# Block-sparse attention with a gated convolution behind it: the same operations in another written order

## The chip, the core and the metric

The kernel runs on one core of a Trainium2 chip. The core has five engines that run at the same time, each of them its own instructions in the order in which they were written: TensorE (PE in the profile; its weight loads are listed as PEld), VectorE (DVE), ScalarE (ACT), GpSimd (POOL) and SyncE (SP). TensorE multiplies matrices and writes to PSUM; VectorE and ScalarE read PSUM and compute; GpSimd writes constants and starts loads; SyncE starts transposing transfers and stores. Engines wait for each other only where one needs the data, or the buffer, of another. The metric is the device time of the whole program in microseconds (us).

## The reference

q, k and v have the shape (4, 8, 768, 64): 4 batches, 8 heads, 768 tokens, 64 values per head. The sequence is cut into 24 blocks of 32 tokens.

```python
scores = scale * np.matmul(q, k.transpose(0, 1, 3, 2))          # scale = 1 / sqrt(64)
mask = np.abs(blk_i - blk_j) <= 1
mask = mask | (blk_i == 0) | (blk_j == 0) | (blk_i == 23) | (blk_j == 23)
for qb in range(24):
    for kb in sampled_blocks[qb]:                               # 3 of them
        mask[qb*32:(qb+1)*32, kb*32:(kb+1)*32] = True
attn = softmax(np.where(mask, scores, -1e9))                    # written out in the reference
x = (attn @ v).transpose(0, 2, 1, 3).reshape(4, 768, 512)       # the heads side by side
h = np.maximum(x @ w_in, 0.0)                                   # 512 -> 1024
conv_out[t] = sum over k of conv_w[k] * h[t + k - 1]            # 3 taps, each channel by itself
out = h * sigmoid(conv_out) @ w_out                             # 1024 -> 512, float32
```

## The kernel before

**Attention.** The mask is not added to the scores but multiplied in with them: a tile T (`t` in the profile) holds, for two heads, the transposed q and k in 64 rows and 24 more rows that encode the mask, so that one matmul over 88 rows gives the masked score. Two heads are a *pair*; there are 16 pairs, four per batch. Attention is cut into 144 *units* of 8 blocks of 128 × 128 scores. For each unit TensorE makes the scores (L755, into one of two PSUM buffers `st`), ScalarE takes the exponential (L767, `pt<-st`, 1024 columns, six `pt` buffers), and TensorE multiplies with V, which has a column of ones beside it for the row sum (L792, into one of two buffers `av`). When the four or so units of a pair are done, VectorE takes the reciprocal of the row sums (L700, `rcp<-av`) and normalizes (L702, `xtok<-av,rcp`), and the tokens are transposed into `xT`.

**Feed-forward.** The tokens are worked on in segments of 384 (the last one as 256 and 128). For each segment and each of eight groups of 128 channels TensorE multiplies with w_in (L889, `mix<-xT,winb`, into one of two PSUM buffers `mix`), and the relu takes the result out of `mix`, on ScalarE (L909) or on VectorE (L911). VectorE makes the three taps (L947 and L955), ScalarE the tanh that serves as sigmoid (L994), VectorE the gate (L997 and L1002). Then TensorE multiplies with w_out (L824, `mix<-woutb,gT`), the result is copied to `o2s` by ScalarE (L327) or VectorE (L331), and SyncE stores it. The work of the feed-forward for one segment is strewn among the units of the next, so that all engines have both kinds of work all the time; only the last segment has its feed-forward with no attention beside it (the tail). In the last segment the taps are matmuls on TensorE (L966).

**Loading.** GpSimd starts all loads that change float32 into bfloat16 on the way (helper `dma`, L238): k and q into `nat` (four buffers) or `nq` (four), v into `vn` (three buffers). Pairs 0 to 5 are transposed by TensorE; pairs 6 to 15 by transposing transfers that SyncE starts (L596, `stg<-nat`, two `stg` buffers) and then two copies `t<-stg` of 64 × 1536 values each, on VectorE or ScalarE. V is copied from `vn` into its place (`vt<-vn`, VectorE, L331). So that the loads don't all start at once, GpSimd executes small copies between them, called *pace*, which wait for the exponential of a given unit (L407) or for the landing of an earlier load (L666).

**Start.** VectorE zeroes `warm` and `ident` (L222, L223). TensorE runs 13 warming matmuls and then 32 *fill* matmuls of 128 columns (L229), which go between the first real ones and whose results are not used. GpSimd makes an index pattern (L260), the identity matrix (L262, a select over the zeroed `ident`), the same in float32 (L286, L287), the ones column of each of the five V tiles (L359, `vt<-`), and the zeros at both ends of the two `hE` buffers that hold h (L364 and L365).

**Order.** The program is a graph of 1789 operations. Each has a name, the engines on which it can run, and the buffers that it takes; some hold several instructions. The numbers beside them (durations, due times `T(u)`) decide nothing any more: `put_down` reads a string, `ORDER`, and issues the operations in the order written there. An entry is two characters for the operation (its number in base 64), one letter for the engine where there is a choice (P, A, V, G, S for TensorE, ScalarE, VectorE, GpSimd, SyncE), and one character for each buffer that it takes. Waits follow from the tiles that operations share, so a string of another order gives a correct program with other waits:

```python
o = ops[64 * CODE.index(line[x]) + CODE.index(line[x + 1])]
...
if len(engines) > 1:
    e = ENGINES[line[x]]
...
for b in o.allocs:
    b.index = CODE.index(line[x])
...
    o.fn(e)
```

Of the kernel before, what the change touches and what calls it, by code (L numbers as in the profile page):

```python
# [25 lines left out]
2u6x11p6y6c6d1u6h6z16i06C06j26D6k6q2W6r6v6E46w1+V6L11ZV6M4Z4R6A1l2H06B6l16N26Q05VV6R2I6mV6F6G6S52a16H26V16I6W323
6O16P2bV6X06J06+01x6KV6T6/2cV6Uid07041b73174ig11s755ieihifV0d7b0iiA7c2GV17g17h7d1iB22o1ij0iDik7i36Y2pV6Z7l0ilV7
7m712qV727n2767q1iC7rim0781iEin7s033797y07z2v1ioV7a27A47717D12UV37EiJ17e7f7j7F52wV47I03507J2y0iL7k7K17o7N12xV7O
7p2Z7t2AV7u7P3iK7S07T7v22J14WiF4U7U04+4O7+12X14T2KV07/1v7B07CiM7G8027H8303902LV7L7M847QiG3012zV2M17R7w7V8818514V
892NV1y7x7W1ip0iN81iq2OV8a08d01q8eis1iH8f482irVeit368l1iI08687iO8b7X18miuViv07Y8q08n28riP8c7Ziy1iR3iz8s5iTiw3o2  # L30
# [5 lines left out]
adaejV2aias1ap19WatjWjz1jXjAau3ax0jYay3tjDjTaz2aj1jZaqaC1aravak0jEVaD9zjBAaK0alaE0awaLk10aAkr1k3am2aM4aBkf0aP1k2
jUaFaQj+3A2aGk43r4aN0aU0aR5aO4/ksk53Y3D0kgj/k63IaVk03LaS4YaZ14aaTaW4a+k7kt3J2khk8a/5b203Cku3M3b3kiaX3iV3uVkvA13Z
aYba1b42b0aH2bb3jV3Bb1kx1bc33E1kjV33Obf0bg3N3vVkybh0kJ03P0b5kKb70aIbk1kzA10kLVbblbp0bqbm11rb61aJkA13VV1kM03yV2
br4bdbe3Tbx1by3FkNbz2kBkOVbibjbnbobsbC0l92kCA3QbDlbbH1bE5kG0b8kS1kTlab9bIkV1kUAbM0bNbJ1kWbtkD1bA0bu1jgkXkEbO3kk
kHkFVgbR1bBbFkIA3KV3bS4B3bGlcbKbT4bZ0b+l10bLkP0kYkQb/5ldbPbQkl1kZc21lec3bvbUkmc423HVbwbV1c0l2c70c8k+kn3RV13/4y1  # L40
ko3SVkRA2c1cc14bbW0cdc954003GVc5c6k904n2l3kakpA34Cck0bXce4cacbcll44QbY0kb3+k/cm1kcl53W4k0cfcgcp1l01l6cqcu0kdV2
lE1cr0lFlh3kecvcn0li4cco4e1lH0lGAl7cz1cw5cAlklIljlK1cscB4lL48lJV4DcE0llctcFlMA41cxlfcy45cG2cM14om51cNcCcDlv1cO5
kwcR0l8cScHlB0lgcT0lC4dm6m7lwcW1ch0lmcXcic/0d0cJ1lDAlx4lV4cY4lncI1lZ0cPcQcUcVlolp04pd12d71l+d84M0lyl/d93dc0dd4E
m0m8lqde0cZ4jdh1462lrm9lzA0dicKc+lsmam1lA504qd2d3da0ltV1cLdm0dj5lN1mbdnlOd42m2d5dbkqlQ0lPVdr1ludo3lRm3df4fdslSV
dgdt1lT1dkm4dz0dAmd2dlcjlW0dB4melXmfdplUlYAmgdqd6dE14rlVA4mdFmcdudv1dG0dCml0dJ0dKmmmz0dL2mhdDdHdO1dImomAmimndPdM
# [5 lines left out]
oqfB0nLnIfCorfG1fD3osot4JVfHnQfI1frnMnRnSnNV1oufL0fMnTV3nV1fN5fsovnWnUft2nY0ownZnXAfufQ0n+AfRf7fY1fS4fZfz0oh0f81
o80oio51f+0ojo6g10o9okfvo7Ag2oaVfAfEfFg32g61fJolfKnOox3fOg7fPomfToyfU1f/ob0oAocg84gb0ozoe1onofodAgcooogAg0g4g5oB
gd0gj1oT0oF1gkoN1oGoCoHgo0gpgl5g9fV0gaoIoOfWoUgq1oJgefXgt1gfoDguoKgm0gnoEgC0grgDgv2gsoLoVgg2oMoPgE5ghgH1oWgigI
oXA2gwgxgM0gNoQoRV3p30gO4p4gy0oSgzp5gJ34Kp6gV0p7A1oYgWpc1pdgX0p90pagF0gGpbV11peAg+1g/h30px1gKh05gLgA1pypi0h4gBV0
gPpzgQh52gY1pjgR0pApf1pgpkApBgZh1phA4hc1gSh2pCh6hdpF0gT1hh0gUVh7he4po0pGhipHpl1hj3pmpIpppnVdhm1hnpqAh80hv0pJpu1
ho0pDpvpN3hf0hghkpwApr0h9pKhwpE0pspOhlhpptAghA1pPhqhx3ha1hBhr0oZ0pQo+hshbAhC0o/hy1pRhzht1pV1p0pSpWhJ1huVhKp1A2pX
hS0qg1pYpLhL3p2hDqhpTqm0pZqiA0qnpUp+qd1hF2pMhTqoAehX1hGhE0hMqx0hU4qehNqyp/hYq10qfA7hO0hPq2hZ3q0i40hH1qAi5q3qp1
hIA1i62qzq4qqhV1hWh+q5A0qBqj1qsqrqCh/0q6i7hQ0i8qkhRAp8i91i02iaq70i1qlA2qN2q8qF3ib1q9icAqPi21qaqHi3Are1qGqbA2rfqt
rgAqOqcr50qur6qIr81r7Arw0qDrxqvr9qErh1riraAqwrb0qJrj0rcq/1rkrdAqQrm1qKrnrlr0qRry0rB0qLro1qMqSrr0rsrT1rpr1rqrt3rz
rH0qTrurCrvrIrJrAqUrDrKrErLA2rUr2rFA0rN0rVr3A1rWrGqV0rXArMqWrYrOrPrQqXrRVqYrSr4qZA3q+  # L60
"""


# [987 lines left out]
```

## Time and profile before

| | |
|---|---|
| time, median of 3 runs | 208.37 us (207.83 to 209.8) |
| the profiled execution | 208.56 us, of which its span in the profile 206.8 us |
| TensorE busy (matmuls) | 197.9 us, 96% |
| ScalarE busy | 190.5 us, 92% |
| VectorE busy | 183.3 us, 89% |
| GpSimd busy | 59.9 us, 29% |

The span is from the first to the last instruction that the profile shows; the program's own time is 1.76 us longer. Times inside the profile count from the start of the span. The views used below are: the page (shares and the chain that ended last), the stretches (busy time of each engine between two points of time; the columns are the stretch, its length, PE, PEld, DVE, ACT, POOL with numbers of instructions, the granted TensorE clock, the share of the DMA engines and GB/s), the list of waits (engine, what waited, for what; total us, how often, the longest), the timeline of one engine (start, busy time, engine, line, operation, output and inputs, count; in brackets the idle time before it and what ended it), and the groups of equal instructions (count; busy us and mean ns of one; idle time before them).

### The profile page before, as it was taken

What the parts mean: (1) busy time and instruction counts of PE and PEld (TensorE: products, weight loads), DVE (VectorE), ACT (ScalarE), POOL (GpSimd) and SP (SyncE); (2) the same over time, 40 slices, a digit from 0 to 9 for tenths busy, and PEclk for the clock granted to TensorE, in tenths of its full rate; (3) what the DMA queues carried; (4) which work ended last, traced back from release to release, by engine and by line L of the source; (5) the groups of instructions that cost most, each with busy time, mean ns of one, the idle gap of its engine ahead of it and who ended that gap; (6) DMA issues with size and microseconds to landing.
All of it is one profiled execution on the core that took longest, in us unless ns stands there. A gap on an engine that the chain in (4) does not pass through costs nothing.

```text
span 206.8 us, 6166 instructions
## 1 busy us (share of the span) xinstructions
PE 197.9 (96%) x2397; PEld 143.3 (69%) x2417; DVE 183.3 (89%) x561; ACT 190.5 (92%) x251; POOL 59.9 (29%) x125
## 2 busy tenths in 40 slices
PE   7899999999979999999999999999999999999992
PEld 5688877877647766776666766776657768787761
DVE  6889899999969999699999998999899929999940
ACT  6999999999988999999999998999899988999751
POOL 8793950800890037411956120000000000000000
PEclk9999999999999999999999999999999999999999
DMA  6999999999699995998999911563213030011205
GB/s 154 147 176 151 146 177 196 136 200 172 77 128 194 179 137 74 168 142 198 120 209 194 243 30 38 67 141 104 101 52 92 19 97 34 3 52 54 103 3 203
DMA packets 51113, 25.40 MB, mean 123 GB/s; under 512 B 36780, under 2 KB 48140, under 8 KB 51084
## 3 DMA queue, kind: packets, MB, share of 16 engines
q0 software_dynamic: 20000, 11.24, 44.6%
q1 hardware_dynamic: 30796, 13.46, 32.8%
q8 instruction: 19, 0.31, 0.7%
q10 hardware_dynamic: 288, 0.30, 0.5%
q14 instruction: 10, 0.08, 0.2%
HBM read 23.09 MB, written 6.29 MB: 142 GB/s over the span
## 4 chain that ended last, share of the span: by engine, by line
PE 66%; DVE 14%; ACT 8%; DMA 6%; issue 3%; POOL 1%; SPq 0%; DVEq 0%
PE st L755 20%; PE mix L889 15%; PE mix L824 14%; PE av L792 11%; ACT pt L767 5%; DVE t L331 4%; DVE m L947 3%; DMA stg<-nat 3%; DMA vn<-in_v_dram 3%; DVE hE L911 2%; DVE m L955 2%; PE av L229 2%; ACT t L327 1%; ACT m L994 1%; PE st L824 1%
## 5 line engine op out<-in xcount | busy, mean ns | idle before, releaser
L767 ACT ACTIVATE pt<-st 128x1024 bf16<-128x1024 f32 (+1 forms) x145 | 140.7, 1027 | 5.1 <-PE st L755 4.4
L755 PE MATMUL st<-t 88*128 88x256 bf16 (+2 forms) x600 | 91.6, 268 | 1.5 <-ACT pt L767 0.8
L792 PEld LDWEIGHTS <-pt 128*128 128x128 bf16 x1152 | 55.5, 97 | 14.6 <-issue 0.2
L792 PE MATMUL av<-vt,pt 128*128 128x65 bf16 x1152 | 62.2, 193 | 0.3
L755 PEld LDWEIGHTS <-t 88*128 88x128 bf16 x600 | 48.0, 97 | 20.6 <-issue 2.8
L889 PE MATMUL mix<-xT,winb 128*128 128x384 bf16 (+2 forms) x288 | 54.1, 308 | 1.8 <-DVE hE L911 1.5
L947 DVE TENSOR_SCALAR m<-hE,cw 128x382 bf16<-128x382 bf16 (+2 forms) x192 | 49.0, 316 | 0.4 <-ACT hE L909 0.2
L824 PE MATMUL mix<-woutb,gT 128*128 128x512 bf16 x164 | 46.1, 379 | 0.4
L955 DVE TENSOR_TENSOR m<-m 128x764 bf16<-128x764 bf16 (+2 forms) x64 | 33.6, 532 | 0.4
L889 PEld LDWEIGHTS <-winb 128*128 128x128 bf16 x288 | 23.7, 97 | 9.6 <-issue 2.4
L994 ACT ACTIVATE m<-m 128x764 bf16<-128x764 bf16 (+2 forms) x32 | 26.3, 826 | 0.1
L824 PEld LDWEIGHTS <-gT 128*128 128x128 bf16 x208 | 17.6, 97 | 10.0 <-issue 0.2
L407 POOL COPY pace<-pt 1x1 bf16<-1x1 bf16 x24 | 6.8, 284 | 44.6 <-ACT pt L767 44.4
L909 ACT ACTIVATE hE<-mix 128x384 bf16<-128x384 f32 (+2 forms) x38 | 18.7, 501 | 1.1 <-PE mix L889 1.0
L1002 DVE TENSOR_TENSOR gT<-m,hE 128x764 bf16<-128x764 bf16 (+3 forms) x36 | 18.0, 510 | 1.0 <-ACT hE L909 0.7
L702 DVE TENSOR_TENSOR xtok<-av,rcp 128x384 bf16<-128x384 f32 (+2 forms) x36 | 18.1, 507 | 0.4
L911 DVE TENSOR_SCALAR hE<-mix 128x384 bf16<-128x384 f32 x26 | 14.2, 552 | 3.9 <-PE mix L889 3.6
L238 POOL DMA_DIRECT2D nat<-in_q_dram x23 | 17.1, 744 | 0.7 <-issue 0.5
L238 POOL DMA_DIRECT2D vn<-in_v_dram x16 | 11.7, 733 | 9.2 <-DVE rcp L700 4.7
L238 POOL DMA_DIRECT2D nat<-in_k_dram x15 | 10.8, 724 | 11.5 <-DMA stg<-nat 7.7
L331 DVE COPY t<-mix 64x384 bf16<-64x384 bf16 (+1 forms) x30 | 12.2, 418 | 0.6 <-ACT t L327 0.2
L997 DVE TENSOR_SCALAR m<-m 128x764 bf16<-128x764 bf16 (+3 forms) x36 | 11.8, 337 | 0.4 <-ACT m L994 0.3
(79 smaller groups left out, 121.2 us busy)
## 6 DMA issues: line engine op xcount, KB each, us to landing
out_dram<-o2s SPq DMA_DIRECT2D x23, 256.0 KB, 2.5
vn<-in_v_dram POOLq DMA_DIRECT2D x16, 192.0 KB, 5.6
nat<-in_k_dram POOLq DMA_DIRECT2D x15, 192.0 KB, 5.8
nat<-in_q_dram POOLq DMA_DIRECT2D x6, 192.0 KB, 6.5
winb<-in_moe_w_in_dram POOLq DMA_DIRECT2D x2, 512.0 KB, 10.0
woutb<-in_moe_w_out_dram POOLq DMA_DIRECT2D x4, 256.0 KB, 7.5
nat<-in_q_dram POOLq DMA_DIRECT2D x9, 96.0 KB, 5.5
nq<-in_q_dram POOLq DMA_DIRECT2D x6, 96.0 KB, 5.1
```

The costliest lines, as they stand in the source:

```text
L238: return op(name, {eng: occ}, lambda e: on(e).dma_start(out=dst(), in_=src), prio, deps, dma=(kind, service), **kw)
L331: nc.vector.tensor_copy(out=dst, in_=src)
L755: nc.tensor.matmul(out=st[:, 128 * x:128 * (x + n_)], lhsT=t[0:88, 12 + 6 * hh + kc, :], rhs=t[0:88, idx:idx + (n_ - 1) * (2 if P < NPE el ...
L767: nc.scalar.activation(out=pt_t[ptb.index][:, c0:c1], in_=st_t[stb.index][:, c0:c1], func=AF.Exp, bias=0.0, scale=0.125)
L792: nc.tensor.matmul(out=o[:, off:off + 65], lhsT=pt_t[ptb.index][:, 128 * x:128 * x + 128], rhs=V_t[vslot_b[P].index][:, hh, kc, 0:65], sta ...
L824: nc.tensor.matmul(out=acc(), lhsT=gT_t[gb.index][:, ffc, 128 * t:128 * t + 128], rhs=woutb[:, ffc, c0:c1], start=(ffc == 0), stop=(ffc == ...
L889: nc.tensor.matmul(out=mix_t[hb.index][:, w1 * y:w1 * y + w1], lhsT=winb[:, fc, 128 * ffc:128 * ffc + 128], rhs=xT_t[xt_buf[n].index][:, f ...
L909: nc.scalar.activation(out=dst, in_=src, func=AF.Relu, bias=0.0, scale=0.5)
L911: nc.vector.tensor_scalar(out=dst, in0=src, scalar1=0.5, scalar2=0.0, op0=ALU.mult, op1=ALU.max)
L947: nc.vector.tensor_scalar(out=m_t[cb.index][:, x, y, 0:w], in0=hE_t[heb.index][:, f0 + y, t0 + x:t0 + x + w], scalar1=cw[:, x, f0 + y:f0 + ...
L955: nc.vector.tensor_tensor(out=m[:, a_, :, 0:w], in0=m[:, a_, :, 0:w], in1=m[:, b_, :, 0:w], op=ALU.add)
L994: th = [op("tanh", {"ACT": t_act(2 * w) + 0.04}, lambda e, cb=cb, w=w: nc.scalar.activation(out=m_t[cb.index][:, 0, :, 0:w], in_=m_t[cb.in ...
```

## The change

Only the string `ORDER` differs: the same 1789 operations in another order, with other engine letters in 22 of them and other buffer numbers. In each engine's own sequence, 729 of TensorE's 894 operations stand at another place than before, 193 of ScalarE's 252, 372 of VectorE's 441, 108 of GpSimd's 118 and 8 of SyncE's 84; most of them by a few places.

What the entries say, where it can be put in words:

- GpSimd's start. Before: identity, index pattern, three ones columns, first k load, two more columns between the first loads, and the zeros of `hE` after the loads (at 7.34 and 15.92 us). After: one ones column (`1c`), index pattern (`0R`), identity (`0S`), zeros of the first `hE` (`1h`), a ones column, zeros of the second `hE` (`1i`), a ones column, and then the first k load (`1P`); the two other columns follow behind that load.
- TensorE's start. Eight more of the fill matmuls stand ahead of the first real ones.
- Around 60 us on VectorE. Before: reciprocal, two copies of transposed q, the copy of pair 8's V (`3mV`), normalization (`96`), two relus (`jmV`, `jjV`). After: reciprocal, normalization, the two copies of q, the first relu, pair 8's V, the second relu. The V copy of pair 7 (`3aV`) moves from 51.5 us to a place near 46.5 us.
- Around 54 us on GpSimd. The pace copies stand elsewhere: between the V loads of pairs 11 (`3U`) and 8 (`3l`) there were a load and four of them, and there are a load and two. The pace copy that waits for the exponential that ends at 48.27 us (`3b`) stood ahead of both loads and comes after them; the next such one (`3e`, for the one that ends at 51.74 us) stood between them and comes ahead of both.
- Engines. Six relus go from VectorE to ScalarE and six the other way; three output copies go to ScalarE and four to VectorE; one copy `t<-stg` (`4v`, for pair 14, near 143 us) goes from VectorE to ScalarE; two copies of `xT` change places.
- The tail. The last w_out products of the last tokens come in another order; one 512-column and one 128-column output copy go from ScalarE to VectorE there.

The diff replaces all 40 lines of the string; shown are the first two lines, those around 60 us (the fourth of them is where `3mV` and `jmV` have changed places), and the one with `4v`:

```diff
 ORDER = """
-0M0N0L00010210S0O030R040V1f0P051e1c1P3060Q07081d090W0a12V0T11A0b1N00c0d0U0e1Q1z00X16A2d21F10Y1AA01g1H01/10Z0+A
-1GA0f0/V10A2111IV5401BA55117V1C0563221h15V14575a01DV5b1EA1R05c21OV30g5f11SV10h1U10i5800j5g182f31VA0k0l595k05h15l
...
-9i03x19j38V8M1j89k52P1949b0j9V09c9n19g4919ojfA237V9hjk19p33p2C09509s02EV9tjl2DV3n4P9u29A14X3mV03X09B96jh0ji3g1
-9C4jmV3d9F0jjV9G9ljq19H1jF09K1979LjGjr9M09mjH9P09QjIjn0ja9R59qjojJ3f39X19YjsVjK9r9v3s09w13w3qjpV9Da00a19Z39x1jN1
...
-mJA04vVf0f4mPA1f50nFfcfj1fkfg1nzmQfdnk1o204wo3nAfl3n/1o4Vo0mKfo0nGo1Afhfp4IV0fq0fw1fxnP0finsfmnHfnnJ1fy2op1nKf60
...
+0M0L001c0R010210N0S0O031h041d1i0V1g0P051P3060Q0712V081e0W090a0T11A0b1f1N00c0d0U0e16A1Q1z00X1F11AA02d21H00Y1GA0f
+0g0h0i1/10/V0+A0Z1BA54121155010A1IV0j0k0l0m0n56317V221C015V575a11DV5b1EA1R1185c55f05g1U01OV00o0p5h00q0r2f31SV10s
...
+je37V9f1939i13k3bj83x18LjfA39jj9V28M19n0502P19o9k2jk038V949b14919cjl9p49509s1963p2C19t2EV9g9h9u39A03X02DV9BjmV
+jh13nji3mV49C13g13d9F1jjV9Gjq09H59ljF09K09L97jG9mjr9M0jH9q9P19QjIja9R29rjn1jJjo3f39vjsV9w09X0jK9YjpV3w3s09D3q9E
...
+n84Hnt3njeY1eZeRnunqn9AjmF1e+2el4uV4eSf10mGnweG2eWf2nB2mL0myf35eHmMmH4inv4vAeXmNeIf90fanxfb3e/mInk0mOfe1nDf0mJA3
...
 """
```

More of the change, by code (lines that the diff above doesn't have):

```diff
@@ L26 @@
[L26 to L30, printed above, removed]
@@ L36 @@
[L36 to L40, printed above, removed]
@@ L41 @@
[L41 to L45, printed above, removed]
@@ L51 @@
[L51 to L55, printed above, removed]
@@ L56 @@
[L56 to L60, printed above, removed]
+0M0L001c0R010210N0S0O031h041d1i0V1g0P051P3060Q0712V081e0W090a0T11A0b1f1N00c0d0U0e16A1Q1z00X1F11AA02d21H00Y1GA0f
@@ new lines @@
+6H06V06I6W6O16P6X46J06T6+16KV6/2Iid17037301b1l74ig0ih7511pie7b1ifV157ciiA3237g07d26U7hiB16Y1x6Zij1iC7i4ik71iD7l1
+727miEilAb2o07q07n07riFim1762qVin7s57827y12pV337zioV7707e7f7A3797j7D07EiJ27a22v04V1v7F1iK7k7o7p7I12wV44W7t3907u
+iG3502xV2y17J7N04+7O522zV7K04S2J04T2AV3017B17C2KV07G2Zip17P54PiM7S14R1y7Tiq2LV7U47H7+02X1irVi7v07/7L7MiH7Q8017R
+8317w847ViL2M17x8527W08802OV89is0iN7X18a381itiI18d1iuV8286iO8e8l02NV87iR08b8c8f5iy08miS36iv17Y8n18q1iU8riz8giP
+8s07Z8v02UV08wiAV8h8o18p8x3iQiw8t1q8A13428BixAcjb08C48F03aV3iT8GiZ38u8y8zj518H5iV8N1i+jciWi/8O8S08i28Dj08P28Tj6
@@ new lines @@
+kr1k3aP0aQalaM03A2aFkgk4am2ks3IaR13zk53YaU1aGaN1j/aVk6aO3r4aZ0k03L4aaSa+aW4aTkh3D0k73C3J2ktaH1k8a/2b213M3b3aXki
+b413jV3iVba0ku3E1kjA2aYbbaIkvV0b0bf1bc33ZkJ01rb1bg3Okx13Bbh2b5bk03vVbl3Nb60bdbm4kybe3uVbp1bikzV00bq3P0kK3Tbr1b72
+bx0b8bykM13yV0kNkLA3aJbC1bjkOVbDbz2bnbol91bsbtkA0bu0bE5kBbvbH0bIkCVkG1bJ4lbkH3FbA0labM1bBbNkIAlcbFbR0bO2bS3QkV0
+bGkD0kWkEbT5bKkXbLbZ1b9kYkFAdb+kS1bPbQb/1kT3KV13VV3c20l12jgc3bUldkkkl0kUAc40l3c71bwc8kP13HV4B3kQc943GVbV1c0cc0
+4y1c1l2c5lecdck14bkZc6clce3cakm3RV1knl4kRA4cbcp0cm5bW13SVcqkolh3k91400kpA2lj45ka4n2cr1bXcu1cfkb3Wlf4Ck+likccg3/
@@ new lines @@
+cn03+kdA3cvk/lE0cw2l5coke4k0lFlH1lkl014e1cz04clGAcAl6cE1ch0cs4DlgctcxlK0bY0cB0llcy48lL4ol7cFlMVlIcG5cCcM0l8cNcD
+lJVlB041cO1lCcicR1m50cSlDAlv1m6kwcT3cW0cXlZ2cHcI1lwl+cY44pcPm8cQcUc/1m7d0lmlp04lV2lxm9d104M0d70lqlnlomad84jcVm0
+4d4Ed93dc1lrmbcJ2cZdd462c+mclsde24qlyl/d2d3ltV3lzA1dh0didm1cKlAlQ1dndj4d41cLm1da0lRdo0d5lN04mdr0lSVlOkqm2dbdslPV
+dz1lT1ludt14fmd0dAdfdgmedklUdB2mfdllW0cjm3lXmglVAdE0dFm4lYAdpdJ1dG4dqdKmhd6mz1duml1dL0mAmmdO0dw2mnmidv1dCdPmodD
+dHdIdMdQ5dW1mjmt0mpmumkmq4x4YdNdX42V244dRdSdY3mBd/0mr47V4e0mvdT0mse11e41dUe5mCe65dZ14Ae90mDV14reamweb443Vee1mR1
@@ new lines @@
+fS4oh0fY0fZfvoio50o9f+5ojo6okg11nOg2o7AoaVfEg60g32fFoloe0g7ox1fJfKomfOozoffPoyg80fTfU0gb1onf/ob1oAocogAfV0gcoo
+odAgj0gkoBgd1g0g4g5oF2oT0oGoN1gl3g9go1oIgpoCgaoHoOfWgq5oJgeoUfXgfgm1oDgngt0oKgugg1oEgC1gDgrgv2gsoLoMoPoVgE5ghgw
+gH0oWgigIoXA1oQgM1gJ1oRV0p304KgNp4gO3oSp5oYp6gxgV0p7A3gy1pc1gzgWg+1p90gX2papdpbV0bg/peAgF1gGh30h05px2gKh4gA1gLpz
+pf0gPgBA0pygQgY0h51pggR0pApi1pjphA6pBhc1pkAhdgSgZh1pChh0pF3gT0pl1pGhe2h2h6h7gUVpmh82pHhipnA3po0hm1hj0h9pDhnpppE1
+hf1hgpIpqApr1psho5pN2pu0pOpvptAhhv0pPhwpwAhkpJhlhx4hA1hBhphqoZ1pQpV0pKha0o+hr0hshbAo/pRhC5ht0hy0pXhJ0hKhuVp0pSpW
@@ L61 @@
+hzqg0p1A0pYhDhE1pThL2qhp2pLpZhF0qm1hS1qiA0hTpUqnp+hGhX0qx2qd0qoA2qyqepMhU4q11p/hYqAqfAchMq0hNq2hZ1qp3i41hH0i5qz
+q3i65hO2hIV1hV0q4hPqrhWh+qN1q5A0qj0i00qqh/1q6i7hQ1i8qBqkhRAp8i92q71qlAfi1qsq8iaqtib0q9icAqCqPqF0i20qai3AqHre0
+qbA1qDrfqOrgAqcr51qGr6quqEr80r9qIr7Arw1rxqvraArh0qwriry2rb0qJrcrj3rzqKq/1rm1rkrlrnrdAr0ro3qLqQrr0rsrprH0qMrT1rB0
+rqqRrt3qSrurUrCrIrvr1qTrArJqUrVrKrDrLA2rWrErXVrN0rOrFA0rPrQr2rGqV0r3V3rMqWrRVrYqXrSqYr4qZA1q+
 """
```

21 lines of the change are left out of this document (11 added, 10 removed).

## The prediction, on record before the result

> **What bounds the kernel now.** The page comes first: which engine is busy, and for how much of the span.
>
> ```profile
> span 206.8 us, 6166 instructions
> PE 197.9 (96%) x2397; PEld 143.3 (69%) x2417; DVE 183.3 (89%) x561; ACT 190.5 (92%) x251; POOL 59.9 (29%) x125
> ```
>
> TensorE leads, but ScalarE and VectorE are close behind, and the busy shares are means over stages. So I cut the span where its character changes, and leave out the start (to 30 us) and the tail (from 190): loading beside both parts of the work (to 60), a stall, steady work with loads (to 140), steady work without.
>
> ```profile
> 30.00:60.00 30.00, 29.55 (x397) 22.07 (x399) 27.84 (x84) 29.77 (x35) 13.35 (x30) 1.00 1.22 152
> 60.00:64.00 4.00, 2.45 (x29) 1.72 (x28) 3.44 (x11) 2.43 (x4) 1.74 (x4) 1.00 1.35 185
> 64.00:140.00 76.00, 75.19 (x919) 53.26 (x925) 72.33 (x209) 73.81 (x93) 23.11 (x47) 1.00 0.92 141
> 140.00:190.00 50.00, 49.65 (x575) 35.23 (x579) 44.87 (x146) 47.97 (x67) 0.00 (x0) 1.00 0.18 56
> ```
>
> From 30 to 60 ScalarE has 0.23 us to spare in 30 (29.77 busy). From 64 to 190 TensorE has 1.16 us to spare in 126 (75.19 + 49.65), ScalarE 4.22. So from 64 on the end is set by the work that TensorE has left, and what brings TensorE to that point sooner moves the end. The granted clock is 1.00 throughout. What remains is the stall at 60 to 64: 2.45 us of TensorE in 4.00. The list of waits says who waited:
>
> ```profile
> ACT pt L767 <- PE st L755: 4.4, 10, 1.6
> ...
> DVE hE L911 <- PE mix L889: 3.6, 3, 2.3
> DVE o2s L331 <- ACT o2s L327: 3.3, 1, 3.3
> ...
> DVE vt L331 <- DMA vn<-in_v_dram: 1.8, 1, 1.8
> ...
> PE mix L889 <- DVE hE L911: 1.5, 1, 1.5
> ```
>
> TensorE's one long wait is the last: a product with w_in needs a `mix` buffer that a relu on VectorE has not emptied. VectorE around it:
>
> ```profile
> 57.12 0.75 DVE L331 COPY t<-stg 64x1536 bf16<-64x1536 bf16 x1
> 57.80 0.17 DVE L700 RECIPROCAL rcp<-av 128x6 f32<-128x6 f32 x1
> 58.01 0.72 DVE L331 COPY t<-mix 64x384 bf16<-64x384 bf16 x2
> 60.52 0.36 DVE L331 COPY vt<-vn 128x768 bf16<-128x768 bf16 x1 [1.79 <-DMA vn<-in_v_dram]
> 60.80 0.55 DVE L702 TENSOR_TENSOR xtok<-av,rcp 128x384 bf16<-128x384 f32 x1
> 61.27 1.02 DVE L911 TENSOR_SCALAR hE<-mix 128x384 bf16<-128x384 f32 x2
> ```
>
> The copy of pair 8's V waits 1.79 us for its load, and the normalization and both relus stand behind it. TensorE's weight loads and ScalarE then stand dry:
>
> ```profile
> 61.87 0.10 PEld L889 LDWEIGHTS <-winb 128*128 128x128 bf16 x1 [1.64 <-issue]
> ```
>
> ```profile
> 57.39 3.87 ACT L767 ACTIVATE pt<-st 128x1024 bf16<-128x1024 f32 x4
> 62.83 1.97 ACT L767 ACTIVATE pt<-st 128x1024 bf16<-128x1024 f32 x2 [1.57 <-PE st L755]
> ```
>
> TensorE loses 1.64 us (from 60.23, which is 61.87 − 1.64), ScalarE 1.57. GpSimd had issued that load at 54.92, behind pace copies, and the chain shows 5.58 us until it landed:
>
> ```profile
> 52.15 0.78 POOL L238 DMA_DIRECT2D vn<-in_v_dram  x1 [3.57 <-DVE vt L331]
> 52.93 0.36 POOL L407 COPY pace<-pt 1x1 bf16<-1x1 bf16 x1
> 53.23 0.77 POOL L238 DMA_DIRECT2D nq<-in_q_dram  x1
> 54.01 0.48 POOL L666 COPY pace<-vn 1x1 bf16<-1x1 bf16 x1
> 54.55 0.43 POOL L666 COPY pace<-nat 1x1 bf16<-1x1 bf16 x2
> 54.92 0.71 POOL L238 DMA_DIRECT2D vn<-in_v_dram  x1
> ```
>
> ```profile
> 54.92 5.58 DMA vn<-in_v_dram
> ```
>
> **The change, part by part.** *The stall.* In the new order VectorE has behind the reciprocal: normalization, two copies, relu `jm`, then pair 8's V. By the rows above that is 57.97 + 0.55 + 0.72 + 0.51 = 59.75 us for the end of the first relu, before TensorE asks for the buffer at 60.23. For the load: the V copy of pair 7, for which the POOL row of 52.15 waited 3.57 us, stands some 5 us earlier, so that wait goes; what holds GpSimd next is the pace copy `3e` (the row of 52.93), now ahead of both loads. Its exponential is the first of these two:
>
> ```profile
> 50.66 1.99 ACT L767 ACTIVATE pt<-st 128x1024 bf16<-128x1024 f32 x2
> ```
>
> It ends at 51.7. From there on GpSimd has two pace copies (0.36 and 0.48), a load (0.78), a load (0.77) and two pace copies (0.37, from 54.55 to 54.92) ahead of pair 8's V, which gives 54.5 us, 0.4 sooner. It lands at 60.1, so the V copy, ready to start at 59.75, waits 0.3. What is late next is the second relu: 60.1 + 0.36 + 0.51 = 61.0, while TensorE is filling the buffer that the first relu freed. So the whole 1.64 us goes: **−1.64**. Bounds: 0, if the next wait takes its place, to −1.64.
>
> *Engines.* The prices, from the groups of equal instructions:
>
> ```profile
> L909 ACT ACTIVATE hE<-mix 128x384 bf16<-128x384 f32 x30 | 14.7, 503 | 0.3 <-PE mix L889 0.3
> ...
> L327 ACT COPY o2s<-mix 128x512 f32<-128x512 f32 x14 | 8.1, 594 | 2.0 <-PE mix L824 2.0
> ...
> L327 ACT COPY t<-t 24x768 bf16<-24x768 bf16 x1 | 0.8, 828 | 0.0
> ...
> L327 ACT COPY t<-mtok 24x384 bf16<-24x384 bf16 x1 | 0.5, 508 | 0.0
> ```
>
> ```profile
> L331 DVE COPY t<-stg 64x1536 bf16<-64x1536 bf16 x20 | 11.5, 581 | 0.3
> ```
>
> Relu `il` goes to ScalarE near 32 us, where ScalarE has 0.23 us to spare: 0.50, less part of that: **+0.4** (bounds 0 to 0.5). The eleven other relus cancel to one more on VectorE later on, where it has 3.67 us free in 76. The staged copy `4v` is 0.58 on VectorE. On ScalarE no row shows 1536 columns; the two copy rows give 0.32 us for 384 columns more, so 0.83 + 2 × 0.32 = 1.47 us, an estimate (bounds: 0.58, VectorE's row, to 1.66, twice the 768-column row). One output copy more than before stands ahead of the last exponential on ScalarE, 0.59. Together 2.06 us, while ScalarE has 2.03 us free from 140 to 190 and 2.19 in the 76 us before. Idle time is never in the right place entirely, so I charge **+0.3** (bounds 0 to 2.06, all of it).
>
> *The start.* Ahead of the first k load stand three ones columns as before, and now the four zeroings of `hE` too.
>
> ```profile
> 1.61 0.83 POOL L238 DMA_DIRECT2D nat<-in_k_dram  x1
> ...
> 7.34 0.23 POOL L364 MEMSET hE<- 128x8 bf16 x1
> 7.38 0.23 POOL L365 MEMSET hE<- 128x8 bf16 x1
> ```
>
> ```profile
> 8.17 0.38 PEld L458 LDWEIGHTS <-nat 128*128 128x128 bf16 x6
> ```
>
> ```profile
> nat<-in_k_dram POOLq DMA_DIRECT2D x2, 192.0 KB, 5.3
> ```
>
> A pair of zeroings takes 0.27 us (7.34 to 7.61), so two pairs 0.54; the index pattern and one of the ones, moved ahead of the identity, run in its wait for the zeroed buffer, so the load is issued 0.3 to 0.5 later. The first two k loads take 5.3 us in the median, so the first lands at about 6.9, and TensorE reads it at 8.17: 1.3 us of slack cover the delay, **0**. Uncovered, with each following load late too, it would be 0.6; with fills and mask copies in worse order, 1.2: bounds 0 to 1.2. The eight fills put ahead cost nothing by themselves, since the same 32 run in the same stage.
>
> *The rest.* SyncE's eight moves pass one transposing transfer behind one store, whose readers come several units later: 0. The tail's order of w_out products has the same last product: 0, bounds −0.6 to +0.6, one 512-column copy. The hundreds of moves by a few places have no price in the trace; they can remove or add waits of the kind in the list. ScalarE's other waits for scores come to 4.4 − 1.57 = 2.8 us; I take **0** and keep −2.8 to +2.8.
>
> *Sum.* 208.56 (the profiled execution; span 206.8 and 1.76 around it) − 1.64 + 0.4 + 0.3 = 207.6. The profiled execution is 0.19 above the median of 208.37, so **207.4 us**.
>
> *A rule that speaks against it.* The trace of before has VectorE copying bf16 in SBUF (57.12, 0.75 us, above) within the 5.58 us of that load. The Trainium skill, page "SBUF — State Buffer", section "SBUF: two separate sides", says that a load issued by GpSimd stands still while VectorE runs a copy of the kind that holds both ports that they share, because its descriptors can't be written. By that rule an earlier issue under such a copy would bring no earlier landing, and the second rival below would be the result. By that rule the time would be 209.1. The trace does not bear it out as a strong effect here: the median over all 16 V loads on the page is no shorter than this one's 5.58.
>
> ```profile
> vn<-in_v_dram POOLq DMA_DIRECT2D x16, 192.0 KB, 5.6
> ```
>
> **Rivals.** *ScalarE becomes the bound* (the slower side). ScalarE sets the pace from 30 to 60 already. If it does so later too, then taking TensorE's wait away only lets ScalarE queue up, the −1.64 brings nothing, and the work added to it, 2.06, is on the path whole: 208.37 + 2.06 = 210.4. It decides from the point where ScalarE's free 2.03 us (140 to 190) are used up, that is from the staged copy at about 143 us on. With the free time partly used it would be 209.3; with relu `il` and a score wait on top, 211.2. For it: 92% busy, 47.97 of 50. Against it: its idle time there is as long as the work added, and TensorE's is 0.35.
>
> *The V load stays late.* If pair 8's load is delayed by VectorE's copies at 56.40 and 57.12 (0.69 + 0.75 = 1.44), it lands at 61.5; the second relu and all behind it wait, and the gain is gone: 208.37 + 0.7 = 209.1. Against it: the 5.58 and 5.6 above.
>
> ```profile
> 56.40 0.69 DVE L331 COPY o2s<-mix 128x512 f32<-128x512 f32 x1 [0.41 <-PE mix L824]
> ```
>
> *More waits go than the one.* If the new order takes away half of the 2.8 us of ScalarE's other waits for scores as well, and the engine changes are covered: 208.37 − 1.64 − 1.4 = 205.3. For it: VectorE's waits of 3.6 and 3.3 in the list are of the same making, an instruction that stands ahead of others and isn't ready. Against it: TensorE has only 1.16 us left to gain from 64 to 190.
>
> *The change does only what its words say*, zeroing ahead of a load that has 1.3 us of slack: 208.4. It lies in the forecast's own range and has no chance of its own.
>
> **How the numbers follow.** Chances: forecast 0.41 (own range 206.1, stall gone and 0.6 in the tail, to 208.5, half of the stall left and both charges); ScalarE bound 0.33; load late 0.11; more waits gone 0.15. Range 205.2 to 211.2: from the third rival's time to the first one's far end; outside lie the ends of the "rest" and of the start, 2 in 10. About 1% (2.1 us) is what a measurement of this kernel can tell from no change, so faster means below 206.3 and slower above 210.4. Slower: half of the first rival (0.17), a little of the second where the start's 1.2 is added (0.03), and of the bounds (0.06): 0.26. Faster: most of the third rival (0.13) and the low end of the forecast (0.06): 0.19. The rest, 0.55, is within.
>
> **What would show it.** In the profile after: no wait of VectorE for a V load near 60 us, and no gap of 1.6 us in TensorE's weight loads there, while the end moves by as much. That V load issued near 54.5 and landing near 60.1. A `t<-stg` row on ScalarE, once, near 143 us, of about 1.47 us; ScalarE's waits for scores from 140 to 190 shorter, not TensorE's waits for `pt` longer. The first k load issued near 2 us, the first real matmul on it still near 8.2. What would make the prediction wrong: TensorE's busy time from 64 to 190 below 98% of the stretch, ScalarE's near 100%, or a new long wait on VectorE in front of relus.

## The result, and the profile after

Over 20 executions each, the changed kernel takes 207.61 us in the median and the kernel before 208.86. The ratio is 0.9952, with a 95% interval of 0.9933 to 0.9971: about 1.0 us faster, clear of noise. The medians are over all executions, while each ratio is over the fast ones alone (here it leaves out 211.35 us of the changed kernel, for one), so it is not just the quotient of the medians, which would be 0.994. The forecast of 207.4 against 208.37 is a ratio of 0.9953. The profiled execution took 207.06 us.

First the page, and the stretches of the span as before (the columns are explained ahead of the prediction):

```profile
span 205.2 us, 6186 instructions
## 1 busy us (share of the span) xinstructions
PE 198.2 (97%) x2398; PEld 142.9 (70%) x2417; DVE 184.4 (90%) x561; ACT 190.8 (93%) x251; POOL 60.8 (30%) x125
```

```profile
30.00:60.00 30.00, 29.75 (x403) 22.22 (x404) 28.93 (x86) 29.89 (x36) 14.95 (x31) 1.00 1.10 153
60.00:64.00 4.00, 4.00 (x61) 3.03 (x59) 3.93 (x13) 4.00 (x6) 1.71 (x5) 1.00 1.47 178
64.00:140.00 76.00, 75.41 (x898) 52.69 (x906) 72.44 (x209) 74.11 (x92) 22.03 (x42) 1.00 0.93 142
140.00:190.00 50.00, 49.68 (x570) 35.41 (x575) 44.81 (x147) 47.68 (x68) 0.00 (x0) 1.00 0.19 59
```

The stretch from 60 to 64 us is the one that changed: TensorE and ScalarE are now busy for all of its 4.00 us (2.45 and 2.43 before). From 64 to 190 the busy times of TensorE, VectorE and ScalarE are the same within 0.3 us in each of the two stretches. The span is 1.6 us shorter, which is the gap that TensorE had at 60.2.

VectorE's timeline there (start, busy time, operation):

```profile
56.69 0.56 DVE L331 COPY t<-stg 64x1536 bf16<-64x1536 bf16 x1
57.17 0.18 DVE L700 RECIPROCAL rcp<-av 128x6 f32<-128x6 f32 x1
57.38 0.56 DVE L702 TENSOR_TENSOR xtok<-av,rcp 128x384 bf16<-128x384 f32 x1
58.04 0.72 DVE L331 COPY t<-mix 64x384 bf16<-64x384 bf16 x2
58.69 0.54 DVE L911 TENSOR_SCALAR hE<-mix 128x384 bf16<-128x384 f32 x1
59.15 0.34 DVE L331 COPY vt<-vn 128x768 bf16<-128x768 bf16 x1
```

The first relu ends at 59.23, ahead of TensorE's request, and the V copy behind it doesn't wait: no bracket stands in its row. ScalarE runs seven exponentials without a pause where it had stood for 1.57 us:

```profile
56.20 6.87 ACT L767 ACTIVATE pt<-st 128x1024 bf16<-128x1024 f32 x7
```

GpSimd issues the load of pair 8's V at 54.73, 0.2 us sooner than before; the trace has it landing at 58.45, 3.7 us later, where it had taken 5.58:

```profile
51.65 0.27 POOL L407 COPY pace<-pt 1x1 bf16<-1x1 bf16 x1 [10.51 <-ACT pt L767]
...
54.73 0.71 POOL L238 DMA_DIRECT2D vn<-in_v_dram  x1
```

At the start the first k load is issued at 1.63 us (1.61 before), although four zeroings stand ahead of it:

```profile
1.38 0.13 POOL L364 MEMSET hE<- 128x8 bf16 x1
1.42 0.13 POOL L365 MEMSET hE<- 128x8 bf16 x1
...
1.63 0.83 POOL L238 DMA_DIRECT2D nat<-in_k_dram  x1
```

The rows of the two zeroings show why: they start 0.04 us after each other, each lasting 0.13, so they overlap.

### The profile page after: what moved, and what is told of

It reads as the page before. It is cut to its first block, busy times and chain, and to the rows that moved or that the text cites. A ratio compares the mean times of both kernels' runs of the same rounds, so it can differ in the third digit from the quotient of the medians.

```text
span 205.2 us, 6186 instructions
## 1 busy us (share of the span) xinstructions
PE 198.2 (97%) x2398; PEld 142.9 (70%) x2417; DVE 184.4 (90%) x561; ACT 190.8 (93%) x251; POOL 60.8 (30%) x125
## 4 chain that ended last, share of the span: by engine, by line
PE 61%; ACT 20%; DVE 14%; issue 4%; ACTq 0%
PE st L755 20%; PE mix L824 15%; ACT pt L767 13%; PE mix L889 10%; PE av L792 10%; DVE m L947 4%; DVE t L331 3%; ACT hE L909 3%; DVE m L955 2%; PE av L229 2%; ACT m L994 2%; ACT t L327 1%; DVE hE L911 1%; DVE xtok L702 1%; PE st L824 1%
## 5 line engine op out<-in xcount | busy, mean ns | idle before, releaser
L767 ACT ACTIVATE pt<-st 128x1024 bf16<-128x1024 f32 (+1 forms) x145 | 142.2, 1041 | 2.6 <-PE st L755 1.4
L755 PE MATMUL st<-t 88*128 88x256 bf16 (+2 forms) x600 | 92.7, 267 | 1.1 <-ACT pt L767 0.4
L792 PEld LDWEIGHTS <-pt 128*128 128x128 bf16 x1152 | 56.2, 97 | 15.1 <-ACT pt L767 0.5
L792 PE MATMUL av<-vt,pt 128*128 128x65 bf16 x1152 | 63.5, 193 | 0.1
L889 PE MATMUL mix<-xT,winb 128*128 128x384 bf16 (+2 forms) x288 | 55.3, 307 | 0.1
L824 PE MATMUL mix<-woutb,gT 128*128 128x512 bf16 x165 | 46.5, 379 | 0.6
L994 ACT ACTIVATE m<-m 128x764 bf16<-128x764 bf16 (+2 forms) x32 | 27.1, 847 | 0.0
L909 ACT ACTIVATE hE<-mix 128x384 bf16<-128x384 f32 (+2 forms) x38 | 19.4, 527 | 0.6 <-PE mix L889 0.3
```

The source lines that it names most:

```text
L755: nc.tensor.matmul(out=st[:, 128 * x:128 * (x + n_)], lhsT=t[0:88, 12 + 6 * hh + kc, :], rhs=t[0:88, idx:idx + (n_ - 1) * (2 if P < NPE el ...
L767: nc.scalar.activation(out=pt_t[ptb.index][:, c0:c1], in_=st_t[stb.index][:, c0:c1], func=AF.Exp, bias=0.0, scale=0.125)
L792: nc.tensor.matmul(out=o[:, off:off + 65], lhsT=pt_t[ptb.index][:, 128 * x:128 * x + 128], rhs=V_t[vslot_b[P].index][:, hh, kc, 0:65], sta ...
L824: nc.tensor.matmul(out=acc(), lhsT=gT_t[gb.index][:, ffc, 128 * t:128 * t + 128], rhs=woutb[:, ffc, c0:c1], start=(ffc == 0), stop=(ffc == ...
L889: nc.tensor.matmul(out=mix_t[hb.index][:, w1 * y:w1 * y + w1], lhsT=winb[:, fc, 128 * ffc:128 * ffc + 128], rhs=xT_t[xt_buf[n].index][:, f ...
L909: nc.scalar.activation(out=dst, in_=src, func=AF.Relu, bias=0.0, scale=0.5)
```

## The experiments

Each run is compared with executions of the kernel before on the same chip. To see where a run gains or loses, I took the end of each unit's exponential (L767) from the two traces and subtracted; a shift that stays the same over many of them means that both kernels run alike there. The exponentials are numbered from 0; as the first unit has two, "unit 56" here and in the expectations is the exponential of that number. The table shows these shifts in us against the profile of before, for runs whose order is mostly that of before.

```
unit                          16      52      56      80      84     112     116     144
about, in before (us)         23      61      68      98     103     139     146     189
V behind relu              +0.18   +0.27   -1.53   -1.52   -1.44   -1.52   -1.52   -1.52
V behind relu, stores      +0.16   +0.10   -0.57   -0.57   -0.57   -0.57   -0.57   -0.57
new order, then old        +0.42   +0.44   -1.39   -1.40   -1.40   -1.39   -1.39   -1.40
staged copy on ScalarE     +0.01   -0.08   -0.75   -0.76   +0.14   +0.04   +1.52   +1.64
the same, output copy off  -0.05   +0.86   +0.80   +0.80   +0.85   +0.80   +1.79   +1.92
V load late                +0.09   +0.05   +5.14   +5.28   +5.87   +5.78   +5.79   +5.79
start late                 +3.33   +3.39   +2.86   +2.86   +2.86   +2.86   +2.87   +2.87
first load late            +0.24   +0.09   -0.44   -0.45   -0.45   -0.44   -0.45   -0.45
```

**The stall alone, undone on VectorE.** One entry of the old order moved (blanks put in for reading):

```diff
-3mV0 3X0 9B 96 jh0 ji 3g1 9C4 jmV 3d 9F0 jjV
+3X0 9B 96 jh0 ji 3g1 9C4 jmV 3mV0 3d 9F0 jjV
```

> The kernel before with one entry moved: on VectorE, the copy of pair 8's V behind the normalization and the first relu that it stood ahead of. Theory A (the stall at 60 us was worth its whole 1.64 us, and the rest of the new order costs some 0.7): the gap in TensorE's weight loads at 60.2 goes, and the time falls by 1.3 to 1.6 us, a ratio of 0.992 to 0.994, more than the whole change brought. Theory B (the gain of the change lies in the order after 64 us; at 60 another wait takes the place of the one removed): no change, ratio within 0.998 to 1.002.

Measured: 207.59 us against 208.01, ratio 0.9968 (0.9943 to 0.9993): faster, by about 0.7 us and not by 1.3 to 1.6. The profiled execution took 207.04 us, 0.55 less than the median; it is 1.52 us ahead of before from unit 56 on, with nothing given back:

```profile
59.41 0.54 DVE L911 TENSOR_SCALAR hE<-mix 128x384 bf16<-128x384 f32 x1
59.87 0.34 DVE L331 COPY vt<-vn 128x768 bf16<-128x768 bf16 x1
```

In it the load had landed at 59.33, after 4.1 us, so nothing waited. The place was right; the size was that of one execution.

**The stall undone on GpSimd instead.**

```diff
-3U0 ... 3e ... 2B2 ... 51 ... 53 ... 52 ... 3l2
+3U0 3l2 ... 3e ... 2B2 ... 51 ... 53 ... 52
```

The load of pair 8's V (`3l2`) stands right behind that of pair 11 (`3U0`).

> The kernel before with one entry moved on GpSimd: the load of pair 8's V issued right behind that of pair 11, at about 52.9 instead of 54.9 us; VectorE's order as before. Theory A: it lands at about 58.5, VectorE waits 0 to 0.2 us instead of 1.79, and the time falls by 1.3 to 1.6 us as when the relu is put ahead. Theory B: no change. By the rival that VectorE's copies hold such a load up: landing no sooner than 60, so VectorE's wait and the time stay.

Measured: 208.00 us against 208.01, ratio 0.9982 (0.9956 to 1.0008): no change that can be told. The V load landed at 57.9 and VectorE no longer waited for it. But the load of q that it had overtaken (`2B`, into `nq`) now came later, and the transposes of that q on TensorE waited instead, and the copies behind them on VectorE:

```profile
59.42 0.17 PEld L521 LDWEIGHTS <-nq 128*128 128x128 bf16 x3 [1.60 <-DMA nq<-in_q_dram]
```

```profile
59.87 0.72 DVE L331 COPY t<-mix 64x384 bf16<-64x384 bf16 x2 [1.54 <-PE mix L521]
```

In this execution another wait took the place of the first, at about the same size. This execution took 208.91 us, the third longest of the twelve (the shortest took 207.28), so how often the load of q comes late is not shown; nor can the ratio be told from the 0.9968 of the run before. What the profile does show is the difference between the two edits: the load put ahead leaves the relu behind a wait, for another load; the relu put ahead of the waiting copy takes the wait off TensorE's path.

**The two halves of the new order.** Up to the exponential of unit 56 one order, from there the other; buffer numbers fitted at the seam.

```diff
-ORDER = all of the old (or all of the new)
+ORDER = the new up to the exponential of unit 56, then what is left in the old order    (first run)
+ORDER = the old up to the exponential of unit 56, then what is left in the new order    (second run)
```

> The new order up to the exponential of unit 56 (65.6 us in the changed kernel), the old order for all that is left then. Theory A: it holds the gain of the stall and the relu on ScalarE, not the staged copy on ScalarE and the new tail: 1.0 to 1.6 us faster than before, ratio 0.992 to 0.995. Theory B: no change, 0.998 to 1.002.

> The old order up to the exponential of unit 56 (67.6 us in the kernel before), the new order for all that is left then. Theory A: the stall stays, the staged copy on ScalarE is charged: 0 to 0.7 us slower than before, ratio 1.000 to 1.0035. Theory B: all of the gain, ratio 0.995.

Measured: new then old 207.38 us against 208.01, ratio 0.9963 (0.9936 to 0.9989), a little less than theory A's 0.992 to 0.995; old then new 208.12, ratio 1.0004 (0.9974 to 1.0034). The gain lies in the first part. The hundreds of moves behind unit 56, the staged copy and the new tail among them, come to nothing that can be measured.

**The staged copy on ScalarE, in the old order.**

```diff
-mJA0 4vV f0 f4 mPA1
+mJA0 4vA f0 f4 mPA1
```

> The kernel before with one letter changed: the staged copy 4v (pair 14, 143 us) on ScalarE instead of VectorE, all else as before. By the forecast: 0 to 0.3 us slower, ratio 1.000 to 1.0015, a copy of 1.47 us in ScalarE's 2.03 us of free time. By the rival that ScalarE sets the pace there: 1.0 to 1.5 us slower, 1.005 to 1.007.

Measured: 209.90 us against 208.38, ratio 1.0077 (1.0049 to 1.0105): 1.6 us slower. The rival's price, or a little more, and not the forecast's. The rows are of ScalarE, of TensorE's weight loads, of VectorE and again of TensorE's weight loads in that run:

```profile
143.36 1.47 ACT L327 COPY t<-stg 64x1536 bf16<-64x1536 bf16 x1
```

```profile
145.36 0.42 PEld L889 LDWEIGHTS <-winb 128*128 128x128 bf16 x3 [0.72 <-issue]
```

```profile
148.41 0.56 DVE L1002 TENSOR_TENSOR gT<-m,hE 128x764 bf16<-128x764 bf16 x1 [2.41 <-ACT hE L909]
```

```profile
149.02 0.11 PEld L824 LDWEIGHTS <-gT 128*128 128x128 bf16 x2 [0.50 <-DVE gT L1002]
```

The copy takes 1.47 us, and what stands behind it on ScalarE comes that much later. An output copy is the first: it has to empty a `mix` buffer, and the trace has TensorE's product with w_in waiting 0.49 us for it until 145.36 (the weight loads of the second row stand for 0.72). Then come the exponentials and a relu: VectorE waits 2.41 us for the relu (0.68 before), and TensorE for VectorE. In the table the step from unit 112 to 116 is +1.48, the copy's whole duration, and none of it is made up later. (The gain of 0.75 at unit 56 is a shorter stall in this execution; it is lost at 84, where staged transposes landed late.)

**The same with the neighbouring output copy moved off ScalarE,** as the new order has it.

```diff
-mJA0 4vV f0 f4 mPA1
+mJA0 4vA f0 f4 mPV1
```

> The kernel before with two letters changed, as the new order has them: the staged copy 4v on ScalarE and the output copy that follows it there (0.57 us) on VectorE. The staged copy alone made the kernel before 1.6 us slower. If the new order is spared that cost because the output copy makes room: 0.9 us more on ScalarE, 0 to 0.9 us slower than before, ratio 1.000 to 1.0045. If it is spared because other work stands around the copy there: still 1.3 to 1.6 us slower, 1.006 to 1.008.

Measured: 209.99 us against 208.56, ratio 1.0074 (1.0050 to 1.0098): still 1.5 us slower. In the profile the step from unit 112 to 116 is +0.99 instead of +1.48: TensorE's wait of 0.49 us for the output copy is gone, which is just the difference, and the rest stays. The +0.8 that this profile has from unit 28 on arose at 25 us, far ahead of the two letters, and is not their doing.

**The new order with the staged copy and the relu `il` back on VectorE.**

```diff
-iE ilA
+iE ilV
...
-4i nv 4vA eX
+4i nv 4vV eX
```

> The new order with two operations back on VectorE where they stand: the staged copy 4v and the relu il. By the forecast, which charged 0.4 and 0.3 us for them on ScalarE: 0.5 to 0.7 us faster than the new order, a ratio to before of 0.992 to 0.993. If the engine changes cost nothing: as the new order, 0.995. If VectorE is the fuller engine where they stand: slower than the new order, 0.997 to 1.000.

Measured: 208.77 us against 208.38, ratio 0.9967 (0.9926 to 1.0007), no faster than the new order's 0.9952, though the interval alone would still admit the forecast's 0.993. Against the profile of the new order the shifts are +0.15 at unit 28, +0.24 at 32 and +0.25 at 80: without `il` on ScalarE the kernel is not sooner. They are +1.54 at 112, +1.30 at 116 and +1.51 at 132: without the staged copy hardly sooner either. ScalarE's rows say why, those of the new order first, then those of this run:

```profile
136.83 1.96 ACT L767 ACTIVATE pt<-st 128x1024 bf16<-128x1024 f32 x2
138.81 1.47 ACT L327 COPY t<-stg 64x1536 bf16<-64x1536 bf16 x1
140.19 1.01 ACT L767 ACTIVATE pt<-st 128x1024 bf16<-128x1024 f32 x1
```

```profile
98.61 0.59 ACT L327 COPY o2s<-mix 128x512 f32<-128x512 f32 x1 [1.64 <-DMA out_dram<-o2s]
...
141.39 1.02 ACT L767 ACTIVATE pt<-st 128x1024 bf16<-128x1024 f32 x1 [1.06 <-PE st L755]
```

With the copy gone, ScalarE waits 1.06 us for scores just where the copy had stood. In the new order the copy stands in a hole, and TensorE makes the hole: between two sets of scores it has eight products with w_out there, of which these are the weight loads of the first six in the new order:

```profile
137.30 1.02 PEld L824 LDWEIGHTS <-gT 128*128 128x128 bf16 x6
```

TensorE itself is busy all that time, so ScalarE can take longer there at no cost, as long as it would only wait for scores. The hole covers 1.06 of the copy's 1.47 us. Of the 0.4 left over 0.24 shows at unit 116 (+1.30 against +1.54 at 112), and at 132 it is gone. In the old order there was no hole at the copy's place: ScalarE's next wait for scores there is 0.56 us at 149.

The first row of this run shows another thing: ScalarE waited 1.64 us, until 98.61, for a free output buffer, whose store SyncE had behind staged transposes that came late. That is the +1.5 between units 80 and 84, and the reason for the next two runs.

**Stores ahead of the staged transposes.** In the new order three stores (`1232`, `1300`, `1312` by number) moved on SyncE; in the old order the same three, with the V copy behind the relu.

```diff
 SyncE, by operation number
-xb 220 ... xb 232, xb 243 ... out 1232, out 1300 ... out 1312
+out 1232, xb 220 ... xb 232, out 1300, out 1312, xb 243 ...
```

> The new order with three stores moved on SyncE, ahead of staged transposes that they stood behind: one whose rows were ready at 56 us and went out at 91, and two ready at 80.5 that went out at 92 and 105. Theory C (late transposes between 80 and 90 us hold up the stores, so that an output copy on ScalarE finds no free buffer, by 1.64 us in the profile of the run before this with two operations on VectorE, and by 0 in that of the new order; that is a part of the spread of the times): no wait of ScalarE for a store near 97 us, 0.3 to 0.8 us faster than the new order in the median, ratio to before 0.991 to 0.994, and a smaller spread. Rival (the spread comes from elsewhere): as the new order, 0.995.

> The kernel before with four entries moved: pair 8's V behind the first relu on VectorE, and the three stores ahead on SyncE. Theory C with theory A: at least as fast as the whole new order, ratio 0.991 to 0.995. If the new order has a gain beside the stall at 60 us that these four don't give: 0.997.

Measured: in the new order 207.25 us against 208.56, ratio 0.9947 (0.9914 to 0.9979), executions from 206.61 to 209.16; that can't be told from the new order's 0.9952, and the spread isn't smaller. In the old order 208.06, ratio 0.9967 (0.9940 to 0.9995), as the V copy alone. Theory C falls: the wait for a store was there (1.6 us in one profile, 0.5 in two others, none in the eleven left), but it is not what spreads the times. What does is open; a part of it is the V load, below.

The second of these runs shows the stall's other half. Here the V load took 5.65 us, and the first relu stood ahead of the wait, the second behind it:

```profile
59.23 0.54 DVE L911 TENSOR_SCALAR hE<-mix 128x384 bf16<-128x384 f32 x1
60.70 0.36 DVE L331 COPY vt<-vn 128x768 bf16<-128x768 bf16 x1 [0.94 <-DMA vn<-in_v_dram]
60.98 0.56 DVE L911 TENSOR_SCALAR hE<-mix 128x384 bf16<-128x384 f32 x1
```

```profile
64.33 0.85 ACT L994 ACTIVATE m<-m 128x772 bf16<-128x772 bf16 x1 [1.13 <-DVE m L955]
```

TensorE's gap at 60 is gone, and exponentials 53 and 54 end 1.6 us sooner than before; but the taps behind the second relu are late, ScalarE waits 1.13 us for them, and from unit 55 on only 0.57 is left.

**The V load later still, in the old order.** Moved behind the four loads that follow it.

```diff
-... 52 3l2 ... 4S ... 3c3 ... 3k ... 3x1 ... 2P1 ... 491
+... 52 ... 4S ... 3c3 ... 3k ... 3x1 ... 2P1 ... 491 3l2
```

> The kernel before with one entry moved on GpSimd: the load of pair 8's V behind the four loads that follow it, issued at about 58.2 instead of 54.9 us, with VectorE's order as before. If each microsecond that this load is late in front of the relus is a microsecond at the end: VectorE waits about 5 us at 60 instead of 1.79, the gap of TensorE grows from 1.6 to about 4.8, and the time by 2.5 to 3.5 us, ratio 1.012 to 1.017. If the stall was in the shade of another wait, or is made up later: less than 1 us, below 1.005.

Measured: 214.74 us against 208.38, ratio 1.0281 (1.0247 to 1.0316): 5.9 us slower, more than the 2.5 to 3.5 that was expected and more than the 3.5 us by which the load landed later (64.02 against 60.50). TensorE's weight loads and VectorE, then the stretches of that run (the tenth column is the granted clock):

```profile
65.39 0.10 PEld L889 LDWEIGHTS <-winb 128*128 128x128 bf16 x1 [5.12 <-issue]
```

```profile
64.04 0.36 DVE L331 COPY vt<-vn 128x768 bf16<-128x768 bf16 x1 [5.27 <-DMA vn<-in_v_dram]
```

```profile
60.00:64.00 4.00, 0.37 (x7) 0.26 (x5) 0.00 (x0) 1.30 (x2) 2.03 (x6) 0.87 1.33 157
64.00:66.00 2.00, 0.61 (x3) 0.27 (x3) 1.92 (x5) 0.00 (x0) 0.00 (x0) 0.50 1.62 180
66.00:68.00 2.00, 2.00 (x13) 1.24 (x12) 1.97 (x8) 0.92 (x1) 0.00 (x0) 0.50 1.62 207
68.00:70.00 2.00, 2.00 (x13) 1.18 (x12) 0.85 (x2) 1.25 (x3) 0.00 (x0) 0.56 0.85 228
70.00:74.00 4.00, 4.00 (x63) 3.20 (x62) 3.62 (x13) 3.59 (x4) 0.35 (x2) 1.00 0.31 60
```

Behind the gap of 5.12 us the granted clock is 0.50 until 69.75 us, which is 4.4 us after TensorE began again, with 13 matmuls in 2 us where there are 63 in 4 us afterwards. The gap is 3.48 us longer than before, and by unit 56 the run is 5.14 us late. The gap of 1.64 us of before left the clock at 1.00. The Trainium skill, page "TensorE: Matmul & The Clock Gate", section "What's actually happening", gives half the clock after an idle window of about 3.4 us; these two gaps lie on either side of it. In detail the trace differs: here the clock fell at 62.92 us (0.96 granted in the stretch from 62 to 63, 0.50 from 63 on), 2.6 us after TensorE's last matmul had ended at 60.37. So by this trace a gap shorter than 3.4 us is not safe from it.

**The start.** Ten zeroings that nothing needs, of the float32 identity, ahead of the first k load and of the identity's own; and, in another run, the identity ahead and four such zeroings of `hE` between it and the load. GpSimd's start is otherwise that of the new order.

```diff
+        for _ in range(10):
+            nc.gpsimd.memset(identf, 0.0)                      # first run, behind the identity ident
...
+            for _ in range(4 * s):
+                nc.gpsimd.memset(hE_t[s][:, 0, 1:129], 0.0)    # second run, behind the zeros of hE
```

> The kernel before with GpSimd's start in the new order and ten more zeroings of the float32 identity (0.2 to 0.25 us each, not needed) ahead of the first k load, so that it and those behind it are issued some 2 us later. Forecast (1.3 us of slack cover the start): 0.7 us slower at the first use, 0.5 to 2.0 us at the end, ratio 1.002 to 1.010. If the fills and the loads' own queue hide the start altogether: no change. If the start had no slack: 2 us slower or more, from 1.010.

> The kernel before with GpSimd's start as in the new order, the float32 identity ahead of the first k load instead of behind it, and four more zeroings (not needed) ahead of it too, so that the load is issued some 1.1 to 1.7 us later while the identity is not late. Forecast (1.3 us of slack between the load's landing and its first use): 0 to 0.4 us slower, ratio 1.000 to 1.002. If the 2.9 us of the run with ten zeroings came through the load: 1.1 to 1.7 us slower, 1.005 to 1.008.

Measured: the first 212.17 us against 208.38, ratio 1.0176 (1.0127 to 1.0225); the second 209.04 against 208.56, ratio 1.0026 (1.0001 to 1.0052). The rows are of GpSimd and of TensorE's weight loads, of the first run and then of the second:

```profile
1.38 2.97 POOL L266 MEMSET identf<- 128x128 f32 x10
```

```profile
6.05 0.50 PEld L455 LDWEIGHTS mix<-identf,o2s 128*128 128x128 f32 x3 [2.52 <-POOL identf L291]
```

```profile
3.34 0.83 POOL L238 DMA_DIRECT2D nat<-in_k_dram  x1
```

```profile
8.40 0.38 PEld L460 LDWEIGHTS <-nat 128*128 128x128 bf16 x6
```

In the first run the 2.97 us of zeroings came through whole (3.33 us at unit 16, 2.87 at the end), as was expected for a start without slack and not for the forecast. But the first transposes waited 2.52 us for the float32 identity, so this is not the load's slack that was used up; the load landed at 8.27 and was read at 10.79. In the profile of before the same transposes wait 0.20 us, and not for the identity:

```profile
3.73 0.52 PEld L451 LDWEIGHTS mix<-identf,o2s 128*128 128x128 f32 x3 [0.20 <-issue]
```

In the second the load was issued 1.73 us later (3.34 against 1.61), but it took 3.64 us where it had taken 4.67, and so landed only 0.70 us later (6.98 against 6.28). TensorE read it 0.23 us later than before (8.40 against 8.17), and by then it had lain there for 1.42 us. So the load's slack, 1.89 us before, was not used up. The exponentials ran 0.24 us late up to unit 28, but not because of the load; where that comes from, and the 0.5 us in the measured time, which is a little above the 0.4 that was forecast, is not shown. The identity, made by 3.09 us (2.80 and 0.29) and read at 3.73, has 0.6 us of slack, which fits the first run: 2.97 us of zeroings, and the first transposes 2.32 us late.

## Why the prediction was right, point by point

**What bounds the kernel: right.** TensorE lost time at one place, and where that went the end moved with it, 1.6 us in the profiles; of the two halves of the new order only the one that holds that place is faster.

**The stall, −1.64: right in its place and its mechanism, too large as a mean.** The gap is gone, the first relu ends at 59.23 (forecast 59.75) and the load is issued at 54.73 (54.5). It landed at 58.45 where 60.1 was forecast, so the wait of 0.3 us that was left for the V copy did not come. But the 1.64 us rest on a load that took 5.58 us in one execution. In the six profiles that have VectorE's old order there and this load at its old place, TensorE's gap at this place was 1.64, 1.58, 1.40, 0.96, 0.96 and 0.83 us: 1.23 in the mean, with loads of 4.5 to 5.6 us. The profile that I argued from had the largest. With 1.23 in place of 1.64, less 0.0 to 0.3 for the engines, the sum is −0.9 to −1.2; measured −1.0. That the sum came out right so closely, at −0.96, is owed to a gain and a charge that were both too large: luck, as far as the number goes.

What I had not seen is that the relu put ahead is only half a cure. With a late load the second relu is still late, as the run with the load of 5.65 us shows, and the V copy behind the relu alone gave a ratio of 0.9968. Whether the other move, on GpSimd, adds to that can't be told from the times (0.9952, with overlapping intervals). In the four profiles that have the new order of GpSimd up to there and the new order of VectorE, the load took 3.6 to 4.1 us and VectorE did not wait for it; in the eight with the old order of GpSimd around it, 4.1 to 5.7. Why the same load is faster there isn't shown: it is issued 0.2 us sooner at most, in one of the four 0.2 us later, and no run separates the pace copies from the other transfers of that time.

**Relu `il`, +0.4: wrong.** ScalarE was busy for 29.89 of 30 us with it, but giving it back to VectorE gained nothing. A full engine is not yet the one that is waited for.

**The staged copy, 1.47 us and +0.3: the duration was exact, the charge close for the wrong reason.** I set the 2.06 us of added work against 2.03 us of free time summed over 50 us. That sum decides nothing, as the old order shows, where the same copy costs its whole 1.47 us. What decides is a hole at its place: 1.06 us in the new order, while TensorE works on w_out.

**The start, 0: right; the load's slack was 1.9 us and not 1.3.** The first load landed at 6.28 in the profile of before, where the median of two loads had put it at 6.9. The delay of 0.3 to 0.5 us that this slack was to cover did not come, since the zeroings overlap (0.02 us); the rows of before, which start at 7.34 and 7.38, showed that already, and 0.27 us is the time until the second ends, not what a pair takes up. The number that matters at the start was missing in the prediction: the float32 identity, which the same queue makes behind the load, has only 0.6 us.

**The rest, 0: right as far as it was tested, behind unit 56.** Old then new is 1.0004, with an interval from −0.5 to +0.7 us.

**The rivals.** That ScalarE becomes the bound holds in the old order, from the point that was named (143 us) and with the copy's whole duration on the path (1.6 us measured; 1.0 to 1.5 was expected for the copy alone, and 2.06 with the output copy in the prediction), and not in the new one. That the V load stays late, by VectorE's copies: the traces speak against it. With such a copy of 0.56 us beside it (at 56.69) the load took 3.7 us; and in the run with the load later still it took 5.45 us, from 58.58 to 64.02, while VectorE had nothing but the last 0.2 us of a copy out of PSUM and then stood idle. So the rule of the Trainium skill, page "SBUF — State Buffer", section "SBUF: two separate sides", is not seen at work here; no run was made that tests it by itself. That more waits go than the one: its condition came true and its gain did not. ScalarE's waits for scores fell from 4.4 to 1.4 us over the whole span, so of the 2.8 beside the stall half is gone; but from 64 us on TensorE's busy share is what it was, and that is what sets the end.

Two sums of the prediction are off by a little: half of the stall left and both charges give 208.25 from the median and not 208.5, and the range's lower end of 205.2 was meant to be the third rival's 205.3. Neither touches the outcome.

## What to carry to other kernels

An instruction that can wait for a transfer should stand behind those that other engines wait for, and not in front of them. Issuing that one transfer sooner can just move the wait to the transfer that it overtakes, as in the one profile of it here. What a move of work to another engine costs is read at its place, from whether that engine has a hole there, and not from its free time summed over a stage. A wait for a transfer that one profile shows is one draw: before its size goes into a sum, look at several executions of the same place.
